# One softmax over tokens' logits for eight blocks, formed from a stash of the turned logits

## The chip, the cores and the metric

The kernel runs on one core of a Trainium2 chip. The metric is the device time of one execution in microseconds; lower is better. The inputs lie in the chip's memory when the time starts, and the output has to be there when it ends.

## What is computed

Three layers, one behind the other. Attention with a decay: 4 batches, 8 heads, 576 positions, 64 columns a head; the scores get the difference of running sums of log f, a causal mask, a softmax and the product with v. Then a feed-forward layer on the 2304 tokens of 512 columns, `g = h * sigmoid(1.702 h)` with `h = x @ w_in` (512 to 2048), and `g @ w_out`. Then a layer of soft experts on its output x:

```
logits = x @ phi                          # 2304 x 32
d = softmax(logits) over the tokens       # each slot's weights
slot_input = d.T @ x                      # 32 slots, 4 for each of 8 experts
slot_out = relu(slot_input @ w1) @ w2     # each expert on its own 4 slots
c = softmax(logits) over the 32 slots     # each token's weights
out = c @ slot_out                        # 2304 x 512
```

Everything is float32 on the way in and out. The change concerns `c`, the softmax of each token over the 32 slots.

## The kernel before

The 2304 tokens are 18 blocks of 128 (`NBLK`), taken two at a time as 9 chunks (`NCH`). `attn_items` lists the steps of attention (scores, exponentials, product with v, turning x) with a place and a modelled cost each; the main part (from L1063) runs the feed-forward layer chunk by chunk in `moe_steps`, and behind each of its steps `attend` emits as many attention items as the modelled costs allow. So attention for later chunks and the feed-forward layer of earlier ones stand side by side. Of the whole program a scheduler then draws up one fixed order for each engine from modelled times (L1282); each engine works off its list in order, and semaphores hold an instruction until its inputs and its buffer are there. A tile with one buffer (`bufs=1`) waits until the tile before it on that tag has had its last use.

In attention's later rows (`emit_qk`, L538) TensorE forms scores (L551, L552, L562, L566), VectorE their maximum (L574), ScalarE the exponential (L578) and a half-precision copy (L586), VectorE the remainder of it (L587), and SP issues a DMA that turns the two (`ph`, L591). `emit_pv` multiplies the turned exponentials with v on TensorE (L628 to L630).

In `moe_steps` TensorE forms `hp` (L800 to L802), ScalarE and VectorE make `g` of it (L813, L814), and `turn` transposes g (L756), copies it (L763) and multiplies it by `wphi`, which is w_out times phi (`by_phi`, L778). These sums of a chunk lie in PSUM on the tag "mi", which has one buffer. When a chunk's sums are complete, `slot_steps` begins, and each step of the next chunk's `moe_steps` drives it on to its next `yield`:

1. VectorE copies the sums out as `l4` (L845). TensorE multiplies by `rsum`, which adds up the four partial sums, in two ways into one tile `lg` on the tag "mi": L853 gives the logits turned (`lT`, slots on partitions, tokens on columns; the 32 slots stand four times, once in each quarter of the partitions), and `by_token` (L856) gives them with tokens on partitions, one matmul of 32 columns for each block.
2. The softmax over tokens goes on from `lT` with a running maximum: `nm` (L881 to L884), exponential `dT` (L885).
3. `token_softmax` (L862) forms `c` for the chunk's two blocks from the logits with tokens on partitions: maximum (L865), subtraction (L866), exponential on ScalarE (L867), sum (L869), a small addition and reciprocal (L870, L871), product into `csm` (L873).
4. After three more steps `dT` is turned back (L896, L898) and weighs g into `spart` (L921, L928).

The last chunk is handled a block at a time (`ts` is one block), and its second block (`end`) does `by_token` and `token_softmax` last of all.

When attention is done, its memory becomes a ring of tiles (`ring`), and SP begins to load the expert weights into it (`load_e`, L1051, L1053, L1056); tiles of the feed-forward layer join the ring as they come free. After the last chunk, `slots_in` (L942) multiplies the slot sums by w_out (L954). `ct_steps` (L979) turns `csm` eight blocks at a time; the first two parts of it are made ahead. `zi` (L1139), the reciprocal sums of the slots, has the tag "rm", two buffers, like the maxima of `token_softmax`; it is read by the ReLU of L1179. The experts' second product `so` (L1194, L1207) uses two PSUM tiles, the second of them on the tag "mi" (L1187), cleared by VectorE (L1189). L1240 multiplies it with the turned `c`, and the output leaves by DMA.

Of the kernel before, what the change touches and what calls it, by code (L numbers as in the profile page):

```python
# [10 lines left out]
F32 = mybir.dt.float32  # L11
# [3 lines left out]
AF = mybir.ActivationFunctionType  # L15
ALU = mybir.AluOpType
AX = mybir.AxisListType
# [13 lines left out]
def attention_moe_softmoe(ctx, tc, q, k, v, f, w_in, w_out, phi, w1, w2, out):  # L31
    nc = tc.nc
# [4 lines left out]
    NS = phi.shape[1]  # L37
# [11 lines left out]
    NCH = NBLK // 2  # L49
# [3 lines left out]
    mp = ctx.enter_context(tc.tile_pool(name="mp", bufs=1))  # L53
# [20 lines left out]
    ident = const.tile([128, 128], F32, name="ident")  # L74
# [16 lines left out]
    zst = const.tile([128, 1], F32, name="zst")  # L91
    spart = mp.tile([128, 512], F32, tag="spart", name="spart")
    csm = const.tile([128, NBLK, NS], F32, name="csm")

    def setup_consts():
        make_identity(nc, ident)
# [730 lines left out]
    def warm(k):  # L827
# [5 lines left out]
        for _ in range(k):  # L833
# [3 lines left out]
                )  # L837
            )

    def slot_steps(c, ts=(0, 1)):  # L840
        fresh = c == 0
        nt = len(ts)
        end = c == NCH - 1 and ts[-1] == 1
        l4 = mp.tile([128, 256], F32, tag="l4", name="l4", bufs=1)[:, 0:128 * nt]
        nc.vector.tensor_scalar(  # L845
            out=l4, in0=P4.pop((c, ts[0]))[:, 0:128 * nt], scalar1=1.0 / (GS * WS), scalar2=None, op0=ALU.mult
        )
        lg = ps_mi("lg")
        lT = lg[:, 0:128 * nt]
        lgv = lg[:, 256:256 + nt * NS].rearrange("p (t s) -> p t s", t=nt)  # L850
# [3 lines left out]
        def by_token():  # L854
            for i in range(nt):
                nc.tensor.matmul(lgv[:, i, :], lhsT=l4[:, 128 * i:128 * (i + 1)], rhs=rsum[:, 0:NS], start=True, stop=True)  # L856

        if not end:
            by_token()
        yield  # L860

        def token_softmax():  # L862
            rm = mp.tile([128, 2, 1], F32, tag="rm", name="rm", bufs=2)[:, 0:nt]
            ee = mp.tile([128, 2, NS], F32, tag="ee", name="ee", bufs=1)[:, 0:nt]
            nc.vector.tensor_reduce(out=rm, in_=lgv, axis=AX.X, op=ALU.max)  # L865
            nc.vector.tensor_tensor(out=ee, in0=lgv, in1=rm.to_broadcast([128, nt, NS]), op=ALU.subtract)  # L866
            nc.scalar.activation(out=ee, in_=ee, func=AF.Exp)  # L867
            rs = mp.tile([128, 2, 1], F32, tag="rs", name="rs", bufs=2)[:, 0:nt]
            nc.vector.tensor_reduce(out=rs, in_=ee, axis=AX.X, op=ALU.add)  # L869
            nc.vector.tensor_scalar(out=rs, in0=rs, scalar1=1e-9, scalar2=None, op0=ALU.add)  # L870
            nc.vector.reciprocal(out=rs, in_=rs)  # L871
            b0 = 2 * c + ts[0]
            nc.vector.tensor_tensor(  # L873
                out=csm[:, b0:b0 + nt, :], in0=ee, in1=rs.to_broadcast([128, nt, NS]), op=ALU.mult
            )


        nm = mp.tile([128, 2], F32, tag="nm", name="nm", bufs=2)
# [7 lines left out]
        if not fresh:  # L886
            nc.scalar.activation(out=nm[:, 1:2], in_=nm[:, 1:2], func=AF.Exp)
        yield
        if not end:
            token_softmax()  # L890
            for _ in range(3):
                yield
        pd = ps_mm("d")
# [7 lines left out]
        if end:  # L901
            sp, pt = (ps_mm("sp"), ps_sc("sp")), (ps_mm("spT"), ps_sc("spT"))
            sT = sums[0] = mp.tile([128, 512], F32, tag="gt", name="sT", bufs=N_GT)
            for n, v in enumerate(halves):
                for fg in range(FG):
                    nc.tensor.matmul(
                        sp[n][NS * fg:NS * (fg + 1), v], lhsT=dd, rhs=G[c, 1, fg][:, v], start=True, stop=True
                    )
            warm(1)
            for n, v in enumerate(halves):  # L910
                nc.vector.scalar_tensor_tensor(
                    out=spart[:, v], in0=spart[:, v], scalar=nm[:, 1:2], in1=sp[n][:, v], op0=ALU.mult, op1=ALU.add
                )
                for a in (2 * n, 2 * n + 1):
                    nc.tensor.transpose(pt[n][:, a * 128:(a + 1) * 128], spart[:, a * 128:(a + 1) * 128], ident)
                (nc.scalar.copy, nc.vector.tensor_copy)[n](out=sT[:, v], in_=pt[n][:, v])
        else:
            sp = ps_mm("sp")
            for i, t in enumerate(ts):
                for fg in range(FG):  # L920
                    nc.tensor.matmul(  # L921
                        sp[NS * fg:NS * (fg + 1), :], lhsT=dd[:, NS * i:NS * (i + 1)], rhs=G[c, t, fg],
                        start=(i == 0), stop=(i == nt - 1),
                    )
            if fresh:
                nc.vector.tensor_copy(spart, sp)
            else:
                nc.vector.scalar_tensor_tensor(  # L928
                    out=spart, in0=spart, scalar=nm[:, 1:2], in1=sp, op0=ALU.mult, op1=ALU.add
                )  # L930
        nc.vector.tensor_copy(nmst, nm[:, 0:1])
        if not fresh:
            nc.vector.scalar_tensor_tensor(
# [2 lines left out]
        yield  # L936
        if end:
            by_token()
            token_softmax()
            yield  # L940

    def slots_in():  # L942
# [121 lines left out]
    if True:  # L1064
# [71 lines left out]
        load_e(KF - 5)  # L1136
        nc.gpsimd.memset(hz, 0.0)

        zi = mp.tile([128, 2], F32, tag="rm", name="zi", bufs=2)  # L1139
        pz = ps_mm("pz")  # L1140
        for hf in range(2):
            for g in range(4):
# [144 lines left out]
```

## Time and profile before

| | us |
|---|---|
| three runs | 566.05, 561.09, 562.74; median 562.74 |
| the profiled execution, its time | 562.1 |
| its span, first to last instruction | 560.4 |
| busy: TensorE, VectorE, ScalarE, GpSimd | 506.8, 354.5, 309.2, 69.0 |
| mean granted TensorE clock, share of full | 0.973 |

The profile is of one execution. Busy time of TensorE is an upper figure, since matmuls are pipelined and their ends are modelled; weight loads (PEld) are listed apart and overlap with matmuls. An instruction on float32 appears in two passes, each with a weight load and a matmul. "Idle before" is the time in which an engine stood still just ahead of an instruction, and "<-" names what released it.

### The profile page before, as it was taken

Reading aid. Unit: us, or ns where it says so; the run is one execution under the profiler, and the core shown is the slowest. Engines: PE = TensorE matmul, PEld = TensorE weight load, DVE = VectorE, ACT = ScalarE, POOL = GpSimd, SP = SyncE. Lnnn points to the kernel's source line nnn. Section 1 sums busy time; section 2 is a strip of 40 time slices with the busy share of each in tenths; the row PEclk is TensorE's granted clock in tenths of the full one; section 3 lists DMA queues with packets and bytes.
Section 4 is the critical chain, followed back from the end, with each engine's and each line's share of the span. In section 5 each row is a group of like instructions: output and inputs, shape, how many; then the busy total and the mean of one; then the engine's idle time right before and its main releaser. Section 6 shows DMA issues by size and latency. Waiting matters only on the chain.

```text
span 560.4 us, 13652 instructions
## 1 busy us (share of the span) xinstructions
PE 506.8 (90%) x5387; PEld 317.4 (57%) x5387; DVE 354.5 (63%) x934; ACT 309.2 (55%) x604; POOL 69.0 (12%) x120
## 2 busy tenths in 40 slices
PE   3566999998989999999999799989999999899991
PEld 3455876775666555665665466546566545454431
DVE  8988969787667357577776667866764413352022
ACT  6767786786767354565666566756564233312111
POOL 4866743310000000000000000000000000000000
PEclk9879799998999999999999899999999999999997
DMA  9997674999867227996759979995544199999999
GB/s 241 275 363 173 171 126 151 262 183 190 153 130 121 58 39 146 181 182 99 130 99 151 154 139 155 208 163 104 85 78 79 37 344 369 363 341 338 379 294 284
DMA packets 229823, 105.63 MB, mean 188 GB/s; under 512 B 202592, under 2 KB 211296, under 8 KB 229760
## 3 DMA queue, kind: packets, MB, share of 16 engines
q1 hardware_dynamic: 228528, 103.59, 80.0%
q10 hardware_dynamic: 1232, 1.18, 0.7%
q8 instruction: 42, 0.69, 0.5%
q14 instruction: 21, 0.17, 0.1%
HBM read 64.63 MB, written 4.72 MB: 124 GB/s over the span
## 4 chain that ended last, share of the span: by engine, by line
PE 70%; DMA 12%; DVE 8%; ACT 5%; issue 2%; SPq 2%; ACTq 0%; DVEq 0%
PE hp L800 10%; PE hp L801 9%; PE hp L802 9%; DMA ph<-pn 6%; PE gT L756 5%; PE p L778 4%; PE pv L623 3%; PE pv L628 3%; PE l L1172 3%; PE sp L921 2%; DMA kf<-in_k_dram 2%; PE scs L551 2%; DMA we<-in_moe_w_dram 2%; PE scs L552 2%; PE pv L630 2%
## 5 line engine op out<-in xcount | busy, mean ns | idle before, releaser
L800 PE MATMUL hp<-w,xt 128*128 128x512 f16 x288 | 110.4, 383 | 0.3 <-DVE spart L928 0.3
L801 PE MATMUL hp<-w,xt 128*128 128x512 f16 x288 | 109.8, 381 | 0.0
L802 PE MATMUL hp<-w,xt 128*128 128x512 f16 x288 | 109.7, 381 | 0.0
L578 ACT ACTIVATE pf<-scs,mx 128x512 f32<-128x512 f32 (+3 forms) x108 | 57.6, 541 | 40.9 <-DVE mx L574 31.7
L814 DVE SCALAR_TENSOR_TENSOR g<-g,hp 128x512 f32<-128x512 f32 x72 | 49.2, 683 | 41.6 <-ACT g L813 40.9
L813 ACT ACTIVATE g<-hp 128x512 f32<-128x512 f32 x72 | 42.6, 591 | 51.6 <-PE hp L802 46.4
L587 DVE SCALAR_TENSOR_TENSOR pn<-pf,pn 128x512 f16<-128x512 f32 (+2 forms) x78 | 51.0, 657 | 31.0 <-ACT pn L586 30.4
L586 ACT ACTIVATE pn<-pf 128x512 f16<-128x512 f32 (+2 forms) x78 | 47.0, 606 | 26.3 <-DMA ph<-pn 25.0
L628 PE MATMUL pv<-vv,ph 128*128 128x65 f16 (+2 forms) x360 | 45.9, 199 | 7.9 <-DMA ph<-pn 7.7
L574 DVE CUSTOM_DVE_ANT_0 scs<-scs,zmq 128x128 f32<-128x128 f32 (+3 forms) x96 | 46.6, 495 | 9.1 <-PE scs L552 6.9
L802 PEld LDWEIGHTS <-xt 128*128 128x128 f16 x288 | 28.3, 98 | 33.3 <-issue 0.6
L763 ACT COPY gt<-gT 128x512 f32<-128x512 f32 x71 | 41.1, 583 | 9.7 <-PE gT L756 9.3
L628 PEld LDWEIGHTS <-ph 128*128 128x128 f16 (+2 forms) x360 | 34.4, 102 | 20.0 <-DMA ph<-pn 10.2
L629 PE MATMUL pv<-vv,ph 128*128 128x65 f16 (+2 forms) x360 | 45.3, 196 | 0.0
L756 PE MATMUL gT<-ident,g 128*128 128x128 f32 x288 | 45.1, 277 | 0.0
L630 PE MATMUL pv<-vv,ph 128*128 128x65 f16 (+2 forms) x360 | 45.1, 195 | 0.0
L800 PEld LDWEIGHTS <-xt 128*128 128x128 f16 x288 | 28.8, 100 | 27.8 <-issue 4.7
L756 PEld LDWEIGHTS gT<-ident,g 128*128 128x128 f32 x288 | 33.9, 142 | 14.4 <-issue 5.0
L801 PEld LDWEIGHTS <-xt 128*128 128x128 f16 x288 | 28.3, 98 | 22.7 <-issue 0.7
L629 PEld LDWEIGHTS <-ph 128*128 128x128 f16 (+2 forms) x360 | 34.7, 103 | 1.9 <-issue 0.2
L551 PE MATMUL scs<-kab,qa 128*128 128x128 f16 x240 | 35.2, 220 | 0.4 <-ACT pf L578 0.4
L585 POOL MEMSET pn<- 128x128 f16 x12 | 2.5, 210 | 267.3 <-DMA ph<-pn 165.8
(226 smaller groups left out, 1036.3 us busy)
## 6 DMA issues: line engine op xcount, KB each, us to landing
we<-in_moe_w_dram SPq DMA_DIRECT2D x127, 256.0 KB, 5.6
raw<-in_moe_w_in_dram SPq DMA_DIRECT2D x16, 512.0 KB, 7.3
raw<-in_moe_w_out_dram SPq DMA_DIRECT2D x16, 512.0 KB, 6.0
kf<-in_k_dram SPq DMA_DIRECT2D x13, 256.0 KB, 3.7
qf<-in_q_dram SPq DMA_DIRECT2D x13, 256.0 KB, 4.1
vf<-in_v_dram SPq DMA_DIRECT2D x12, 256.0 KB, 4.4
out_dram<-ob SPq DMA_DIRECT2D x12, 256.0 KB, 3.2
ph<-pn SPq DMA_TRANSPOSE x78, 3.3
```

Source lines behind the costliest of these rows:

```text
L574: nc.vector.tensor_tensor_reduce(out=o, in0=o, in1=mask, scale=-SC, scalar=3.0e38 if n == 128 else DG[r][1][:, u], op0=ALU.add, op1=ALU.mi ...
L578: nc.scalar.activation(out=pf[:, hh * nb:(hh + 1) * nb], in_=o, func=AF.Exp, bias=mx[:, hh:hh + 1], scale=-1.0)
L586: nc.scalar.activation(out=pn[:, 0, 0:w], in_=pf, func=AF.Copy, scale=PB)
L587: nc.vector.scalar_tensor_tensor(out=pn[:, 1, 0:w], in0=pf, scalar=PB, in1=pn[:, 0, 0:w], op0=ALU.mult, op1=ALU.subtract)
L628: nc.tensor.matmul(o, lhsT=ph[0:rr, 0, off:off + n], rhs=vh, start=(j == 0), stop=False)
L629: nc.tensor.matmul(o, lhsT=ph[0:rr, 0, off:off + n], rhs=vl, start=False, stop=False)
L630: nc.tensor.matmul(o, lhsT=ph[0:rr, 1, off:off + n], rhs=vh, start=False, stop=(j == i))
L756: last_turn[0] = nc.tensor.transpose((pt if a < 2 else pt2)[:, a * 128:(a + 1) * 128], g[:, a * 128:(a + 1) * 128], ident)
L800: nc.tensor.matmul(hp, lhsT=xt[:, 0, kk, ts], rhs=win(0, fg, kk), start=(kk == 0), stop=False)
L801: nc.tensor.matmul(hp, lhsT=xt[:, 0, kk, ts], rhs=win(1, fg, kk), start=False, stop=False)
L802: last_hp[0] = nc.tensor.matmul(hp, lhsT=xt[:, 1, kk, ts], rhs=win(0, fg, kk), start=False, stop=(kk == KD - 1))
L814: nc.vector.scalar_tensor_tensor(out=g, in0=g, scalar=1.0, in1=hp, op0=ALU.add, op1=ALU.mult)
```

## The change

For chunks 0 to 7 the logits with tokens on partitions are no longer made by `by_token`. Instead ScalarE copies one quarter of the turned logits `lT`, 32 partitions by 256 columns, into a tile `stash` of 128 partitions: chunk c into quarter c % 4. After every fourth chunk (c = 3 and 7) `token_softmax_8` turns the stash with two 128x128 transposes, each of which writes its 128 columns in four runs of 32, into one PSUM tile (on the tag "mi" the first time, on "sc" the second), and runs one softmax over all eight blocks. It is emitted behind `spart` of that chunk. The last chunk's two blocks stay as they were. The exponential is now formed in place in `csm`, and the tags "rm" and "rs" have one buffer each, wider than before; `zi`, which shares "rm", has one buffer too. The number of steps that `slot_steps` yields is unchanged.

```diff
--- before.py
+++ after.py
@@ -91,6 +91,7 @@
     zst = const.tile([128, 1], F32, name="zst")
     spart = mp.tile([128, 512], F32, tag="spart", name="spart")
     csm = const.tile([128, NBLK, NS], F32, name="csm")
+    stash = mp.tile([128, 256], F32, tag="stash", name="stash")
 
     def setup_consts():
         make_identity(nc, ident)
@@ -837,9 +838,32 @@
                 )
             )
 
+    def token_softmax(b0, nt, lgv):
+        rm = mp.tile([128, 8, 1], F32, tag="rm", name="rm", bufs=1)[:, 0:nt]
+        ee = csm[:, b0:b0 + nt, :]
+        nc.vector.tensor_reduce(out=rm, in_=lgv, axis=AX.X, op=ALU.max)
+        nc.vector.tensor_tensor(out=ee, in0=lgv, in1=rm.to_broadcast([128, nt, NS]), op=ALU.subtract)
+        nc.scalar.activation(out=ee, in_=ee, func=AF.Exp)
+        rs = mp.tile([128, 8, 1], F32, tag="rs", name="rs", bufs=1)[:, 0:nt]
+        nc.vector.tensor_reduce(out=rs, in_=ee, axis=AX.X, op=ALU.add)
+        nc.vector.tensor_scalar(out=rs, in0=rs, scalar1=1e-9, scalar2=None, op0=ALU.add)
+        nc.vector.reciprocal(out=rs, in_=rs)
+        nc.vector.tensor_tensor(
+            out=ee, in0=ee, in1=rs.to_broadcast([128, nt, NS]), op=ALU.mult
+        )
+
+    def token_softmax_8(b0):
+        pl = (ps_mi if b0 == 0 else ps_sc)("lt")[:, 0:8 * NS]
+        for t in range(2):
+            nc.tensor.transpose(
+                pl.rearrange("p (g t s) -> p t g s", t=2, s=NS)[:, t], stash[:, 128 * t:128 * (t + 1)], ident
+            )
+        token_softmax(b0, 8, pl.rearrange("p (b s) -> p b s", s=NS))
+
     def slot_steps(c, ts=(0, 1)):
         fresh = c == 0
         nt = len(ts)
+        one = c == NCH - 1
         end = c == NCH - 1 and ts[-1] == 1
         l4 = mp.tile([128, 256], F32, tag="l4", name="l4", bufs=1)[:, 0:128 * nt]
         nc.vector.tensor_scalar(
@@ -855,24 +879,12 @@
             for i in range(nt):
                 nc.tensor.matmul(lgv[:, i, :], lhsT=l4[:, 128 * i:128 * (i + 1)], rhs=rsum[:, 0:NS], start=True, stop=True)
 
-        if not end:
+        if one and not end:
             by_token()
+        if not one:
+            gs = slice(NS * (c % 4), NS * (c % 4 + 1))
+            nc.scalar.copy(out=stash[gs], in_=lT[gs])
         yield
-
-        def token_softmax():
-            rm = mp.tile([128, 2, 1], F32, tag="rm", name="rm", bufs=2)[:, 0:nt]
-            ee = mp.tile([128, 2, NS], F32, tag="ee", name="ee", bufs=1)[:, 0:nt]
-            nc.vector.tensor_reduce(out=rm, in_=lgv, axis=AX.X, op=ALU.max)
-            nc.vector.tensor_tensor(out=ee, in0=lgv, in1=rm.to_broadcast([128, nt, NS]), op=ALU.subtract)
-            nc.scalar.activation(out=ee, in_=ee, func=AF.Exp)
-            rs = mp.tile([128, 2, 1], F32, tag="rs", name="rs", bufs=2)[:, 0:nt]
-            nc.vector.tensor_reduce(out=rs, in_=ee, axis=AX.X, op=ALU.add)
-            nc.vector.tensor_scalar(out=rs, in0=rs, scalar1=1e-9, scalar2=None, op0=ALU.add)
-            nc.vector.reciprocal(out=rs, in_=rs)
-            b0 = 2 * c + ts[0]
-            nc.vector.tensor_tensor(
-                out=csm[:, b0:b0 + nt, :], in0=ee, in1=rs.to_broadcast([128, nt, NS]), op=ALU.mult
-            )
 
 
         nm = mp.tile([128, 2], F32, tag="nm", name="nm", bufs=2)
@@ -886,8 +898,9 @@
         if not fresh:
             nc.scalar.activation(out=nm[:, 1:2], in_=nm[:, 1:2], func=AF.Exp)
         yield
+        if one and not end:
+            token_softmax(2 * c + ts[0], nt, lgv)
         if not end:
-            token_softmax()
             for _ in range(3):
                 yield
         pd = ps_mm("d")
@@ -928,6 +941,8 @@
                 nc.vector.scalar_tensor_tensor(
                     out=spart, in0=spart, scalar=nm[:, 1:2], in1=sp, op0=ALU.mult, op1=ALU.add
                 )
+        if c % 4 == 3:
+            token_softmax_8(2 * c - 6)
         nc.vector.tensor_copy(nmst, nm[:, 0:1])
         if not fresh:
             nc.vector.scalar_tensor_tensor(
@@ -936,7 +951,7 @@
         yield
         if end:
             by_token()
-            token_softmax()
+            token_softmax(2 * c + ts[0], nt, lgv)
             yield
 
     def slots_in():
@@ -1136,7 +1151,7 @@
         load_e(KF - 5)
         nc.gpsimd.memset(hz, 0.0)
 
-        zi = mp.tile([128, 2], F32, tag="rm", name="zi", bufs=2)
+        zi = mp.tile([128, 2], F32, tag="rm", name="zi", bufs=1)
         pz = ps_mm("pz")
         for hf in range(2):
             for g in range(4):
```

## Rows read from the trace of the kernel before

**Rows 1.** Stretches: us, busy us (instructions) of each engine, clock, DMA share, GB/s.
```profile
460.00:480.00 20.00, 19.32 (x141) 9.95 (x140) 6.16 (x19) 5.89 (x14) 0.00 (x0) 1.00 1.03 371
...
sum 285.00, PE 277.24 PEld 168.82 DVE 188.61 ACT 166.61 POOL 3.61; mean PE 19.80 PEld 12.06 DVE 13.47 ACT 11.90 POOL 0.26
```

**Rows 2.** SP's queue: timeline (start, length in us), and one of its waits.
```profile
445.77 41.91 SPq L1051 DMA_DIRECT2D we<-in_moe_w_dram  x60
...
502.88 0.33 SPq L1053 DMA_DIRECT2D hz<-in_moe_w_dram  x1
...
SPq L1053 <- PE sw L954: 3.6, 2, 3.2
```

**Rows 3.** Waits of PE between 160 and 445 us: us in total, times, longest.
```profile
PE pv L628 <- DMA ph<-pn: 7.4, 8, 2.0
```

**Rows 4.** Timeline of weight loads around L856 in chunks 2 and 6.
```profile
247.16 0.63 PEld L856 LDWEIGHTS lg<-rsum,l 128*128 128x128 f32 x4
247.63 0.50 PEld L756 LDWEIGHTS gT<-ident,g 128*128 128x128 f32 x4
248.10 0.10 PEld L800 LDWEIGHTS <-xt 128*128 128x128 f16 x1
...
432.93 0.63 PEld L856 LDWEIGHTS lg<-rsum,l 128*128 128x128 f32 x4
433.60 0.10 PEld L630 LDWEIGHTS <-ph 64*64 64x64 f16 x1
```

**Rows 5.** Groups by line and shape: one chunk's softmax (busy us, mean ns | idle before).
```profile
L867 ACT ACTIVATE ee<-ee 128x64 f32<-128x64 f32 x8 | 2.0, 256 | 1.3 <-DVE ee L866 1.3
...
L873 DVE TENSOR_TENSOR csm<-ee,rs 128x64 f32<-128x64 f32 x8 | 1.8, 220 | 0.1
...
L865 DVE TENSOR_REDUCE rm<-lg 128x2 f32<-128x64 f32 x8 | 1.7, 218 | 0.3 <-ACT dT L885 0.3
...
L870 DVE TENSOR_SCALAR rs<-rs 128x2 f32<-128x2 f32 x8 | 1.3, 166 | 0.2
```

**Rows 6.** Groups by line and shape: instructions on 256 columns.
```profile
L885 ACT ACTIVATE dT<-lg,nm 128x256 f32<-128x256 f32 x8 | 3.7, 468 | 9.8 <-DVE nm L883 7.5 <-PE scs L552 2.4
...
L881 DVE TENSOR_REDUCE nm<-lg 128x1 f32<-128x256 f32 x8 | 3.4, 421 | 3.9 <-PE lg L856 3.9
L845 DVE TENSOR_SCALAR l<-p 128x256 f32<-128x256 f32 x8 | 3.4, 419 | 0.9 <-PE p L778 0.9
...
L258 ACT COPY part<-wq 128x256 f32<-128x256 f32 x8 | 2.9, 369 | 1.1 <-PE wq L253 1.0
```

**Rows 7.** The tail: timelines of DVE and ACT, and a wait from 500 us on.
```profile
506.29 0.16 DVE L1148 TENSOR_SCALAR zi<-pz 128x2 f32<-128x2 f32 x1 [1.18 <-PE pz L1144]
506.37 0.18 DVE L865 TENSOR_REDUCE rm<-lg 128x1 f32<-128x32 f32 x1
...
523.71 0.69 ACT L1179 ACTIVATE g<-l,zi 128x512 f32<-128x512 f32 x1 [3.51 <-PE l L1172]
...
PEld so L1207 <- DMA we<-in_moe_w_dram: 2.8, 5, 0.7
```

**Rows 8.** Stretches of 5 us around the largest hole (columns as in rows 1).
```profile
305.00:310.00 5.00, 4.06 (x64) 2.54 (x59) 3.95 (x8) 4.14 (x9) 0.00 (x0) 1.00 0.54 104
310.00:315.00 5.00, 4.40 (x76) 3.00 (x73) 3.17 (x10) 3.42 (x7) 0.00 (x0) 1.00 0.60 116
315.00:320.00 5.00, 3.02 (x32) 1.44 (x31) 3.96 (x9) 1.47 (x3) 0.00 (x0) 0.85 1.23 152
320.00:325.00 5.00, 5.00 (x55) 2.91 (x55) 2.18 (x5) 4.00 (x9) 0.20 (x1) 0.81 1.16 211
```

**Rows 9.** Timeline of DVE behind the sums of chunk 3.
```profile
298.33 0.74 DVE L928 SCALAR_TENSOR_TENSOR spart<-spart,nm,sp 128x512 f32<-128x512 f32 x1
...
305.31 0.69 DVE L587 SCALAR_TENSOR_TENSOR pn<-pf,pn 128x512 f16<-128x512 f32 x1 [2.78 <-ACT pn L586]
```

## Prediction

> **What bounds the kernel now.** I read the busy time by stretches first [rows 1]. Between 160 and 445 us, where the feed-forward chunks and the attention run interleaved, TensorE is busy for 277.2 of 285.0 us; VectorE for 188.6 (66%) and ScalarE for 166.6 (58%). From 460 to 480 us TensorE is still at 19.3 of 20, and DMA now runs at its full share (1.03, 371 GB/s), because the expert weights load. So what is to be asked of every edit is what it does to TensorE's issue, and whether the weight loads behind it let the gain through.
>
> They do, by the queue of SP [rows 2]. The first expert load is issued at 445.77 us, once attention is done. Near the end the queue stops: it waits 3.6 us for the matmuls of L954, and the load behind them goes out at 502.88. L954 can only run when the last chunk's sums are ready, so the loads after 502.88 follow TensorE, not only DMA. A shift of TensorE before 500 us moves both the start of the loads and this stop, and with it the end.
>
> Next the waits of TensorE within 160 to 445 us: the only one that counts is L628 on the turned exponentials `ph`, 7.4 us in 8 places [rows 3]. The rest is issue. TensorE is the bound there, with a few holes.
>
> **The change, part by part.** The sum is made against the profiled execution's own time, 562.1 us (a span of 560.4 and 1.7 around it). The median of the three runs shown is 562.74, 0.6 higher, inside their spread of 5.
>
> *TensorE, removed.* For each of the chunks 0 to 7 the two matmuls of L856 go. Each appears as two passes, so a group has four weight loads. From the first load of a group to the next instruction's load pass 247.63 - 247.16 = 0.47 us for chunk 2 and 433.60 - 432.93 = 0.67 us for chunk 6 [rows 4]. The other six groups read 0.47 five times and 0.67 once. Removed: 6 x 0.47 + 2 x 0.67 = 4.16 us. This is what the weight loads take; 32 columns stream in less.
>
> *TensorE, added.* Two 128x128 transposes for four chunks, four in all. L756 is the same operation: four of them from 247.63 to 248.10, 0.47 us [rows 4]. Added: 0.47 us. From below it is 0, if the loads go beside a running matmul; from above I allow twice the row, 0.94, since no row has a transpose that scatters its output in runs of 32 columns. I take 0.47, the row itself.
>
> The Trainium skill speaks against this part: its page "PSUM — Partial Sum Buffer", section "Specifications (TRN2)", says that any non-contiguous access pattern slows matmuls significantly. It gives no factor, and no row here shows such a write; an estimate by it, with the four transposes taking twice as long, makes the net gain 3.2 us.
>
> Net on TensorE: -4.16 + 0.47 = -3.7 us.
>
> *VectorE.* The softmax of one chunk has two reductions (0.218 us, L865), two elementwise steps (0.220, L873) and two small ones (0.166, L870) [rows 5]: 1.21 us, eight times 9.7 us. The one for eight blocks works on 128x256: reductions as L881 (0.421) and elementwise as L845 (0.419) [rows 6], 2 x 0.421 + 2 x 0.419 + 2 x 0.166 = 2.01 us, twice 4.0. VectorE loses 5.7 us, beside TensorE. I count it as nothing; at best it shortens the holes of [rows 3] (rival A).
>
> *ScalarE.* Eight exponentials of 0.256 us go [rows 5]; two of 0.468 (as L885) and eight stash copies come. A copy has 32 partitions of 256 columns; the nearest row is L258, 0.369 us for 128 partitions of as many columns [rows 6]. In all -2.05 + 0.94 + 2.95 = +1.8 us, on an engine that is 58% busy. The copy stands ahead of the exponential L885 on ScalarE, but L885 itself idles 9.8 us over its eight times, 7.5 of it for the maximum on VectorE [rows 6]; the copy fits there. Without that cover it would delay L885 by up to 0.37 us a chunk, 3.0 in all; I take 0.
>
> *New waits.* First, the turned stash of the first four chunks takes the single "mi" bank, which the running sums of the next chunk (L778) and its logits also need. Whoever comes after it waits for two transposes, one reduction and one subtraction: 0.24 + 0.421 + 0.419 = 1.1 us. Behind a waiting L778 on TensorE stand transposes and feed-forward matmuls that need nothing from it, and the order is drawn up so that ready ones go first. Between 0 and 1.1; I take 0. Before, the same bank was held through the old reads of L865 and L866 in every chunk, so something is given back. Second, the copy of chunk 4 overwrites the stash and must wait for the first two transposes, which are short: 0. Third, the tag "rm" now has one buffer and `zi` uses it. `zi` is written at 506.29 and read until the last L1179 ends, 523.71 + 0.69 = 524.40 [rows 7]. The last block's maximum L865, now at 506.37, would come after it, and its bank is the one that the second half of `so` is cleared in. With three VectorE steps of about 0.2 us (as L865 there) the second half starts near 525.0 instead of 524.2. That 0.8 us is covered: L1207 still waits 2.8 us for weights on the way [rows 7]. If TensorE stood still for the whole last softmax as well (another 1.2 us by rows 5, and the splits), it would be some 2.5 us, just under that cover. I take 0, and keep 2.5 as the end of the range for it.
>
> **Sum:** 562.1 - 4.16 + 0.47 = 558.4; I say 558.5 us. What is late next is the same TensorE stream, 3.7 us earlier.
>
> **The rivals.** A, more is won: VectorE has 5.7 us less to do in the stretches where the chain maximum, exponential, split, `ph` decides. For it speak the 7.4 us of holes [rows 3], and that the worst of them, 305 to 320 us (5 - 4.06, 5 - 4.40 and 5 - 3.02, 3.5 us idle), also brings the granted clock to a mean of 0.85 and 0.81 of 2.4 GHz over the next two 5 us, that is part of the time at 1.2 GHz, some 0.75 + 0.95 = 1.7 us more [rows 8]. Against it: most of these holes end with a DMA, which VectorE only starts. Half of 7.4 + 1.7 won: 558.5 - 4.5 = 554.0.
>
> B, less is won: what the first six chunks save (5 x 0.47 + 0.67 = 3.0) is time in which TensorE arrives earlier at the same holes and waits longer. Then only the last two groups count, 0.67 + 0.47 - 0.24 = 0.9: 561.2. For it: the `ph` of a hole goes through SP's queue among the row loads, which don't move with TensorE. Against it: the scores that begin each of these chains are TensorE's own and come earlier too.
>
> C, slower: the first softmax for eight blocks lands in front of the worst hole. Its place in the program is right behind `spart` of chunk 3, at 298.33 us; on VectorE it takes 0.421 + 0.419, then the exponential's 0.468, then 0.421 + 0.332 + 0.419, 2.5 us from end to end. VectorE waits 2.78 us before the split L587 at 305.31 [rows 9]. Started before 302.8 it fits in; from there on each 0.1 us is 0.1 us of L587, of the `ph` behind it, and of TensorE in the hole. In full: 2.5, the 1.1 of the bank, and once more the 1.7 of lower clock [rows 8]: 558.5 + 5.3 = 563.8. Against it: the four softmaxes before it are gone, so the items arrive earlier.
>
> **How the numbers follow.** My forecast gets 0.50, A 0.20, B 0.15, C 0.15. A run of this kernel can tell about 1% (5.6 us) from no change. Faster by more than that is below 556.5: most of A (0.17) and the low edge of the forecast (0.06), 0.23. Slower by over 1% is above 567.7: only C with a second hole of the same kind (another 5.2 us, 3.5 + 1.7), and what a newly drawn order might do elsewhere: 0.09. The rest, 0.68, is within 1%. The forecast's own range is 556 to 561: doubled transposes and the bank (+1.6), up to 2.5 at the end if its cover goes, and down to where a hole closes. To hold 8 in 10 the range takes in most of A and of C: 553.5 to 565.5.
>
> **What would show it.** L856 down from 36 to 4 passes; L865 to L873 under new lines with four executions each (two wide, two narrow); 32-partition copies of some 0.37 us on ScalarE; the first expert load near 442.5 instead of 445.77, the load after L954 near 499.2 instead of 502.88. If both shift by 3 to 4 us and the end doesn't, the reading of the tail is wrong. If the first load doesn't shift, B is right; if the waits of L628 in 160 to 445 us fall under 4 us, A; if they rise over 10, C. The last maximum should stand after 524 us less the shift, with no wait of L1194 that reaches the output. The prediction is wrong if TensorE's groups were not worth 0.47 us each, which the gap from L853 to its successor would show.

## The result, and the profile after

The changed kernel takes 555.21 us in the median of six runs (551.72 to 558.32), the kernel before 563.48 in six runs beside it. The ratio is 0.9859, with an interval of 0.9829 to 0.9888: faster by 1.4%, that is by 8 us, where I had forecast 3.6 us, a chance of 0.68 for "within 1%" and of 0.23 for more. The profiled execution took 555.42 us, with a span of 553.3. Of the runs below, the profiled ones of e1 and e10 took 590 and 1213 us, where their others took 550 to 563, and one of e11 took 1.6% more than its fastest; these three are left out of all numbers.

The tail did as forecast. Timeline of SP's queue, kernel after; the two rows answer to [rows 2]:

```profile
438.18 1.79 SPq L1066 DMA_DIRECT2D we<-in_moe_w_dram  x4
...
495.19 0.33 SPq L1068 DMA_DIRECT2D hz<-in_moe_w_dram  x1
```

The first expert load goes out 7.6 us earlier, the load behind the stop 7.7 earlier, the span ends 7.1 earlier. So the whole gain was made before 438 us and the tail handed it on. The late maximum of the last block came as described, in the timeline of VectorE (kernel after; [rows 7]):

```profile
516.73 0.19 DVE L844 TENSOR_REDUCE rm<-lg 128x1 f32<-128x32 f32 x1
```

A wait of TensorE after 500 us, kernel after:

```profile
PEld so L1222 <- DMA we<-in_moe_w_dram: 2.9, 5, 0.7
```

It runs at 516.73 instead of 506.37, behind the last ReLU, and `so` still waits for its weights as long as before (2.9 us against 2.8): the cover held.

The new instructions cost what their neighbours did. Groups of the kernel after by line, VectorE's and ScalarE's first; they answer to [rows 4 to 6]:

```profile
L844 DVE TENSOR_REDUCE rm<-lt 128x8 f32<-128x256 f32 x2 | 0.8, 419 | 0.0
L845 DVE TENSOR_TENSOR csm<-lt,rm 128x256 f32<-128x256 f32 x2 | 0.8, 418 | 0.0
L886 ACT COPY stash<-lg 32x256 f32<-32x256 f32 x8 | 2.9, 363 | 5.8 <-PE lg L877 5.8
```

And the transposes of the octets (the softmaxes over eight blocks) beside those of g, with min/median/max in ns (kernel after). Unlike the matmuls of L856, a float32 transpose appears in one pass:

```profile
L858 PEld LDWEIGHTS lt<-ident,stash x4: 138/141/144, 332.9 to 464.8; 128*128 128x128 f32 x4
L858 PE MATMUL lt<-ident,stash x4: 272/272/328, 332.9 to 464.9; 128*128 128x128 f32 x4
...
L757 PEld LDWEIGHTS gT<-ident,g x288: 137/141/224, 109.5 to 486.6; 128*128 128x128 f32 x144
L757 PE MATMUL gT<-ident,g x288: 272/273/329, 109.7 to 486.7; 128*128 128x128 f32 x144
```

Predicted were 0.421, 0.419 and 0.369 us for the first three. Now the stretch of attention, by 5 us, columns as in [rows 1, 8] (kernel after):

```profile
305.00:310.00 5.00, 3.92 (x52) 2.59 (x51) 3.06 (x7) 3.20 (x6) 0.00 (x0) 1.00 0.55 105
310.00:315.00 5.00, 5.00 (x77) 3.20 (x75) 4.02 (x11) 3.60 (x7) 0.00 (x0) 1.00 0.93 134
315.00:320.00 5.00, 5.00 (x90) 3.41 (x88) 3.42 (x9) 3.21 (x7) 0.21 (x1) 1.00 0.75 147
320.00:325.00 5.00, 4.87 (x37) 2.41 (x35) 3.29 (x9) 3.21 (x7) 0.00 (x0) 1.00 1.25 202
```

TensorE's waits between 160 and 445 us, kernel after:

```profile
PE pv L629 <- DMA ph<-pn: 5.1, 5, 1.5
PE hp L801 <- DVE g L815: 0.7, 1, 0.7
PE lg L877 <- DVE l L869: 0.7, 1, 0.7
```

The worst hole of before is gone: 1.2 us idle in these 20, against 3.5, and the clock is whole. But one of 1.5 us stands just behind, at 326 us, where the kernel before has none between 325 and 330. The waits on `ph` fell from 7.4 to 5.1 us, between my marks for rival A (under 4) and rival C (over 10). TensorE's timeline shows that hole and the place of the third wait (kernel after):

```profile
326.36 0.20 PE L629 MATMUL pv<-vv,ph 128*128 128x65 f16 x1 [1.50 <-DMA ph<-pn]
...
377.91 0.70 PE L877 MATMUL lg<-l,rsum 128*128 128x256 f32 x2 [0.72 <-DVE l L869]
```

The third wait is for the sums of chunk 5, and has nothing to do with the first octet, which VectorE's timeline shows some 40 us earlier, behind the sums of chunk 4:

```profile
330.15 0.41 DVE L869 TENSOR_SCALAR l<-p 128x256 f32<-128x256 f32 x1
...
334.02 0.42 DVE L844 TENSOR_REDUCE rm<-lt 128x8 f32<-128x256 f32 x1
...
334.95 0.42 DVE L845 TENSOR_TENSOR csm<-lt,rm 128x256 f32<-128x256 f32 x1
...
338.80 0.41 DVE L851 TENSOR_TENSOR csm<-csm,rs 128x256 f32<-128x256 f32 x1
```

The octet of chunks 0 to 3 did not run behind chunk 3's `spart` (rival C's place) but at 334 us. It is strung out over 5 us between attention's items, so it holds nothing up for 2.5 us at a stretch. Between 327 and 377 us TensorE has no wait of half a microsecond, so the "mi" bank that the octet holds cost nothing to be seen.

**Where the time went.** I cut the span at two instructions that both kernels have: the copy `l4` (L845, after L869) of chunk 0 and that of chunk 7. Stretches, first of the kernel before, then of the kernel after:

```profile
170.03:466.46 296.43, 289.25 (x3105) 173.54 (x3103) 188.43 (x539) 167.24 (x336) 3.61 (x30) 0.99 0.72 134
```

```profile
169.00:458.87 289.87, 283.74 (x3079) 169.74 (x3078) 184.36 (x503) 167.31 (x337) 3.57 (x30) 1.00 0.72 138
```

1.0 us was gained before chunk 0, ahead of every changed instruction; 6.6 between the cuts; 0.5 was given back behind them. Of the 6.6, idle time of TensorE (length less busy) is 7.18 - 6.13 = 1.1. The low clock of [rows 8] cost 3.02 x 0.15 + 5.00 x 0.19 = 1.4 before and nothing after. The rest, 289.25 - 1.4 - 283.74 = 4.1, is work at full clock; forecast for the seven groups between the cuts, less one octet's transposes, was 3.3 to 3.5. So the groups are there, and some 2.5 us come from holes and clock, which the sum had at zero.

### The profile page after: what moved, and what is told of

It is laid out like the page before. It is cut to its first block, busy times and chain, and to the rows that moved or that the text cites. A ratio compares the mean times of both kernels' runs of the same rounds, so it can differ in the third digit from the quotient of the medians.

```text
span 553.3 us, 13559 instructions
## 1 busy us (share of the span) xinstructions
PE 500.3 (90%) x5359; PEld 313.1 (57%) x5359; DVE 350.8 (63%) x898; ACT 310.3 (56%) x606; POOL 69.8 (13%) x120
## 4 chain that ended last, share of the span: by engine, by line
PE 66%; DMA 14%; DVE 9%; ACT 5%; issue 3%; SPq 2%; ACTq 0%; POOL 0%; DVEq 0%; POOLq 0%
PE hp L801 9%; PE hp L802 8%; PE hp L803 8%; PE gT L757 5%; DMA ph<-pn 4%; PE p L779 4%; PE pv L624 3%; DMA we<-in_moe_w_dram 3%; PE pv L629 3%; PE l L1187 3%; PE sp L934 2%; DMA kf<-in_k_dram 2%; PE scs L552 2%; DMA kab<-kan 2%; PE scs L553 2%
## 5 line engine op out<-in xcount | busy, mean ns | idle before, releaser
L757 PE MATMUL gT<-ident,g 128*128 128x128 f32 x288 | 45.0, 276 | 0.0
L629 PEld LDWEIGHTS <-ph 128*128 128x128 f16 (+2 forms) x360 | 34.1, 101 | 18.2 <-DMA ph<-pn 8.0
L757 PEld LDWEIGHTS gT<-ident,g 128*128 128x128 f32 x288 | 34.2, 141 | 14.7 <-issue 4.4
L631 PEld LDWEIGHTS <-ph 128*128 128x128 f16 (+2 forms) x360 | 34.7, 103 | 1.7 <-issue 1.4
L630 PEld LDWEIGHTS <-ph 128*128 128x128 f16 (+2 forms) x360 | 34.5, 102 | 2.0 <-issue 0.2
```

The source lines that it names most:

```text
L629: nc.tensor.matmul(o, lhsT=ph[0:rr, 0, off:off + n], rhs=vh, start=(j == 0), stop=False)
L630: nc.tensor.matmul(o, lhsT=ph[0:rr, 0, off:off + n], rhs=vl, start=False, stop=False)
L631: nc.tensor.matmul(o, lhsT=ph[0:rr, 1, off:off + n], rhs=vh, start=False, stop=(j == i))
L757: last_turn[0] = nc.tensor.transpose((pt if a < 2 else pt2)[:, a * 128:(a + 1) * 128], g[:, a * 128:(a + 1) * 128], ident)
```

## The experiments

The question: does TensorE's term hold when it is the only change, and what opened or closed the holes: the softmax's work on VectorE or ScalarE, its place, the bank, or merely the order that the scheduler drew up? Every edit makes it draw a new one. Ratios are to the kernel before, timed on the same chip; the brackets hold 95% intervals. Each profile is of one execution. Of e1 and e10 only the times are used.

**Matmuls alone (e1, e1b).** The kernel before without the groups of L856; the softmax reads turned logits.

```diff
-        if not end:
+        one = c == NCH - 1
+        if one and not end:
             by_token()
+        if not one:
+            lgv = lg[:, 0:nt * NS].rearrange("p (t s) -> p t s", t=nt)
```

> The kernel before without the matmuls of by_token in chunks 0 to 7; the softmax of these chunks runs with all its instructions on the first 64 columns of the turned logits instead, so c is formed from other numbers there. SP's order differs from before in 2 lines only. Theory 'issue' (the weight loads of the removed matmuls, 0.47 us a group, are time on TensorE; 4.2 us in all): 4.2 us less than before, ratio 0.9925, within 1.5 us. Theory 'relief' (the gain comes from VectorE's shorter work): nearly nothing, under 1 us. Theory 'groups cost more' (the removed matmuls explain all of the change): 7 to 9 us less, ratio 0.985.

> The same kernel as e1_no_matmul, once more for a profile: the kernel before without the by_token matmuls of chunks 0 to 7 (the softmax reads the first 64 columns of the turned logits instead, so the weights of the tokens are other numbers). Theory 'terms': the matmuls are worth their issue time alone, 0.47 to 0.67 us a group, 4.2 us in all, ratio 0.992 to 0.996, and the waits of TensorE on the turned exponentials between 160 and 445 us stay near the 7.4 us of before. Rival 'matmuls close the holes': these waits fall under 4 us and the ratio is near the whole change's, 0.986.

Measured: 0.9952 [0.9919, 0.9986], and again 0.9966 [0.9939, 0.9992]: 1.9 to 2.7 us, the second just past the upper edge of "terms". The stretch between the cuts and two of 5 us (e1b):

```profile
169.70:464.17 294.47, 285.57 (x3077) 170.14 (x3075) 187.04 (x540) 165.70 (x336) 3.57 (x30) 0.99 0.75 135
...
365.00:370.00 5.00, 2.14 (x28) 1.40 (x27) 3.12 (x7) 3.65 (x8) 0.00 (x0) 0.97 1.00 186
370.00:375.00 5.00, 5.00 (x39) 2.67 (x37) 1.94 (x7) 1.83 (x4) 0.00 (x0) 0.68 0.82 108
```

TensorE's waits between the cuts (e1b):

```profile
PE pv L628 <- DMA ph<-pn: 5.4, 6, 1.5
PE scs L551 <- ACT pf L578: 1.6, 2, 1.4
```

Busy time at full clock falls by 3.9 us (285.57 less 1.7 of low clock, against 287.85), which is the forecast of the groups. But idle rises from 7.18 to 8.90: `ph` is waited for a little less (6.8 before), the scores' bank and others more. So by the profile half of it is given back; by the times the gain may be anything from 0.4 to 4.6 us. That is rival B's mechanism, and matmuls alone don't close holes.

**Matmuls back (e3).** The kernel after with the groups in all chunks again, read by nobody.

```diff
-        if one and not end:
+        if not end:
             by_token()
```

> The changed kernel with the matmuls of by_token in all chunks again, their results unused in chunks 0 to 7. Theory 'issue plus order' (3.7 us of the gain are TensorE's issue, the rest comes from the order that the scheduler happened to draw between 283 and 430 us): SP's order is here nearer to that of before (8 lines differ) than to that of the changed kernel (24), so both parts of the gain go: ratio to before 0.995 to 1.003. Theory 'relief' (VectorE's 5.7 us less): only the matmuls' 4.2 us come back, ratio 0.993. Theory 'groups cost more': all of the gain goes, ratio 1.00, by the matmuls alone, and then the run without them has it all.

Measured: 0.9868 [0.9831, 0.9904], below what all three theories had. By this ratio the groups are hardly seen (0.9859 without them, intervals of 0.3% on both sides). But the kernel before got faster in the course of that chip's runs, from 562.8 to 565.6 us in the first seven to 560.1 to 562.1 in the other ten; against the median of all seventeen, e3's median gives 0.9917, and the groups would be worth some 3 us. By the profile they are seen (e3, between the cuts):

```profile
170.34:462.42 292.08, 286.60 (x3107) 173.23 (x3106) 184.94 (x503) 167.65 (x337) 3.57 (x30) 1.00 0.68 136
```

286.60 - 283.74 = 2.9 us for 28 more passes, seven groups of 0.41. Idle is 5.5, less than in the kernel after. So with all the old matmuls in place half of the gain or more stays, and that part hangs on the softmax, not on the groups.

**The softmax's place (e4).** The kernel before, with each chunk's softmax emitted behind its `spart`.

```diff
         if not end:
-            token_softmax()
             for _ in range(3):
                 yield
...
+        if c < NCH - 1:
+            token_softmax()
         nc.vector.tensor_copy(nmst, nm[:, 0:1])
```

> The kernel before with the softmax of each chunk moved in the program from behind the exponential of the turned logits to behind the slot sums; nothing is left out. SP's order is that of before, TensorE's differs in 5 lines. Theory 'issue plus order': no change, ratio 0.998 to 1.002. Theory 'place' (the softmax stood in front of attention's maxima and splits on VectorE, and the changed kernel gains because it no longer does): 2 to 4 us less, ratio 0.993 to 0.996.

Measured: 1.000 [0.997, 1.003]. This change of place makes no difference. Between the cuts, and around the old hole (e4):

```profile
169.64:466.06 296.42, 287.91 (x3105) 173.05 (x3104) 188.65 (x539) 167.16 (x336) 3.57 (x30) 1.00 0.73 134
...
305.00:310.00 5.00, 4.04 (x54) 2.33 (x54) 3.67 (x8) 4.06 (x8) 0.00 (x0) 1.00 0.50 97
310.00:315.00 5.00, 4.40 (x82) 3.21 (x80) 3.36 (x10) 3.38 (x6) 0.00 (x0) 1.00 0.59 113
315.00:320.00 5.00, 2.54 (x44) 1.57 (x39) 3.71 (x8) 1.91 (x4) 0.00 (x0) 1.00 1.11 125
```

The hole of [rows 8] is there again, 4.0 us against 3.5, but at full clock.

**The bank (e8).** The kernel after, with the turned stash in the "mm" bank both times.

```diff
-        pl = (ps_mi if b0 == 0 else ps_sc)("lt")[:, 0:8 * NS]
+        pl = ps_mm("lt")[:, 0:8 * NS]
```

> The changed kernel with the turned stash in a bank of the tag mm (three buffers) both times, instead of the single bank of mi and one of sc; nothing is left out. SP's order here is nearer to that of before (12 lines differ) than to that of the changed kernel (26). Theory 'issue plus order': the direct part stays, 3.7 us, the part that came with the order goes, ratio to before 0.992 to 0.995. Theory 'relief': the work is that of the changed kernel, ratio 0.986. If the wait for the single bank in chunk 4 cost something in the changed kernel, this one is faster than it by up to 1.1 us.

Measured: 0.9866 [0.9823, 0.991], against 0.9859. The 1.1 us that I had allowed for the "mi" bank cannot be seen.

**VectorE's steps alone (e9), ScalarE's alone (e10).** The kernel after with six more VectorE steps of a chunk's softmax in each of the chunks 0 to 7, or with its exponential, written to scratch.

```diff
+        if not one:
+            lv = lg[:, 0:nt * NS].rearrange("p (t s) -> p t s", t=nt)
+            nc.vector.tensor_reduce(out=rx, in_=lv, axis=AX.X, op=ALU.max)
+            nc.vector.tensor_tensor(out=ex, in0=lv, in1=rx.to_broadcast([128, nt, NS]), op=ALU.subtract)
+            nc.vector.tensor_reduce(out=ry, in_=ex, axis=AX.X, op=ALU.max)
...
```

```diff
+        if not one:
+            nc.scalar.activation(out=ex, in_=lg[:, 0:nt * NS].rearrange("p (t s) -> p t s", t=nt), func=AF.Exp)
```

> The changed kernel with six more VectorE instructions a chunk in chunks 0 to 7, of the kinds, the sizes and the place of the old softmax, on the turned logits, into a tile that nobody reads; no exponential. TensorE's and SP's orders stay close to those of the changed kernel (4 lines of SP's differ). Theory 'relief', by VectorE: 3 to 4.5 us of the gain go, ratio to before 0.992 to 0.994. Theory 'order': the time of the changed kernel, ratio 0.985 to 0.988.

> The changed kernel with the eight exponentials of 64 columns on ScalarE again, at the old place, into a tile that nobody reads. SP's order is that of the changed kernel. Theory 'relief', by VectorE, and theory 'order': the time of the changed kernel, ratio 0.985 to 0.988. Theory 'relief', by ScalarE: 2 to 4 us of the gain go, ratio 0.990 to 0.993.

Measured: e9 0.988 [0.984, 0.9919], e10 0.9812 [0.9762, 0.9861]. Eight more exponentials take nothing away. VectorE's steps take 1.2 us by time, with some 2.8 either way; the one profiled execution has more (e9, between the cuts and two stretches of 5 us):

```profile
169.36:462.83 293.47, 285.01 (x3079) 170.19 (x3078) 189.24 (x545) 167.56 (x337) 3.56 (x30) 0.99 0.71 135
...
220.00:225.00 5.00, 2.91 (x47) 2.00 (x46) 3.13 (x7) 3.29 (x7) 0.20 (x1) 1.00 0.74 137
225.00:230.00 5.00, 5.00 (x34) 2.48 (x32) 2.21 (x5) 1.56 (x4) 0.20 (x1) 0.66 0.90 196
```

Idle is back to 8.5, and a hole of 2.1 us is followed by 1.7 us of low clock. The profile suggests "relief" by VectorE, but the times lie below its 0.992 to 0.994, at the edge of "order".

**Everything back (e11).** The kernel after with the matmuls and the whole softmax chain, exponential included, in the chunks 0 to 7 beside the new octets. It is e3 plus the chain.

```diff
-        if one and not end:
+        if not end:
             by_token()
...
+        if not one:
+            nc.vector.tensor_reduce(out=rx, in_=lgv, axis=AX.X, op=ALU.max)
+            nc.vector.tensor_tensor(out=ex, in0=lgv, in1=rx.to_broadcast([128, nt, NS]), op=ALU.subtract)
+            nc.scalar.activation(out=ex, in_=ex, func=AF.Exp)
+            nc.vector.tensor_reduce(out=ry, in_=ex, axis=AX.X, op=ALU.add)
...
```

> The kernel after with all that the change took out put back beside the new: both matmuls of by_token and the whole softmax chain over VectorE and ScalarE in each of the chunks 0 to 7, written to a scratch tile. Theory 'work': the removed work as a whole made time and holes, so everything gained is lost: ratio 0.999 to 1.004, waits on the turned exponentials back to 6 us or more. Theory 'order': only TensorE's groups come back, 3.5 us, and the holes stay as small as in the kernel after unless the order drawn up puts others there: 0.988 to 0.994.

Measured: 0.9994 [0.9961, 1.0027]. All that was gained is lost again, as "work" has it, though the waits on `ph` (below) stay under the 6 us that I had named with it. From e3 to e11, where TensorE's matmuls are the same, that is 1.26%, 7 us, with some 2.8 either way (4 us by the plain medians). The stretch between the cuts (e11):

```profile
170.46:465.29 294.83, 286.20 (x3107) 173.35 (x3106) 189.66 (x546) 169.67 (x345) 3.57 (x30) 1.00 0.72 135
```

TensorE's waits there (e11):

```profile
PE pv L629 <- DMA ph<-pn: 5.6, 6, 1.5
PE scs L552 <- ACT pf L579: 1.0, 2, 0.7
```

TensorE's work is e3's (286.2 against 286.6); its idle time goes from 5.5 to 8.6. Work and idle time together are 2.7 us more than in e3. The profiled execution was 1.3 us faster than e11's median, and that of e3 0.9 slower than its own, so they show less of the loss than the times.

**No softmax (e2, e2b), and nothing at all (e7, e7b).** The kernel before without the softmax of chunks 0 to 7; the kernel after without stash and octets. Both need `csm` filled with something: by GpSimd at the very start in e2 and e7, by one VectorE step at chunk 8 in e2b and e7b.

```diff
-        if not end:
+        if c == NCH - 1 and not end:
             token_softmax()
+        if not end:
             for _ in range(3):
```

```diff
-        if not one:
-            gs = slice(NS * (c % 4), NS * (c % 4 + 1))
-            nc.scalar.copy(out=stash[gs], in_=lT[gs])
...
-        if c % 4 == 3:
-            token_softmax_8(2 * c - 6)
```

> The kernel before with its matmuls of by_token, but without the per-chunk softmax over tokens in chunks 0 to 7 (48 instructions on VectorE, 8 on ScalarE; csm is zero there). Theory 'relief' (the gain beyond TensorE's own 3.7 us comes from the softmax work that leaves VectorE and ScalarE): 4 to 7 us less than before, ratio 0.988 to 0.993. Theory 'order' (it comes from the order that happens to be drawn): this one has an order of its own, 38 lines of SP's differ from before, and the ratio may lie anywhere from 0.990 to 1.005.

> The changed kernel without the stash copies, the four transposes and the two softmaxes of eight blocks: chunks 0 to 7 have no softmax over tokens at all, csm is zero there. What the added parts cost is the difference to the changed kernel. Theory 'issue plus relief': the transposes' 0.5 us and a share of 4.0 us of VectorE, 1 to 3 us less than the changed kernel, ratio to before 0.980 to 0.985. If the added parts are hidden altogether: ratio 0.985 to 0.988.

> As e2_no_softmax (before without the softmax of chunks 0 to 7, matmuls kept), but the rows of csm are filled at chunk 8 by one VectorE instruction from spart, not at the start by GpSimd, so that the first 170 us are those of before. Theory 'relief' (VectorE's and ScalarE's softmax work makes the holes): the chunk sums of chunk 0 to 7 come closer together by 3 to 4 us and the ratio is 0.990 to 0.994. Theory 'order' (holes go with the order drawn up, not with the work): holes of the size of before somewhere, ratio 0.997 to 1.006, and the loss of e2 from chunk 0 on shows again. If e2 was slow only by its first 170 us: below 1.002.

> As e7_none (neither matmuls nor softmax nor stash for chunks 0 to 7), filled at chunk 8 by VectorE. If e7's first 170 us were lost to its GpSimd fill alone: ratio 0.981 to 0.986, the whole change's or a little less, since the octets' own work is 0.5 us of TensorE. If the fill had no part in it: 0.993 to 0.995 as e7. Less than 0.981 would say that the octets and stash copies cost more than their rows.

Measured: e2 1.0105 [1.0076, 1.0134] and e7 0.9941 [0.991, 0.9972], with chunk 0's `l4` at 175.0 and 176.3 us instead of 170.0 and 169.0. With the fill at chunk 8 instead, e2b is 0.9998 [0.9969, 1.0026] and e7b 0.98 [0.9747, 0.9854], the fastest kernel here along with e10. So e2b loses little in its first 170 us (chunk 0's `l4` at 171.6) and yet gains nothing, against "relief". Between the cuts and two stretches of 5 us (e2b):

```profile
171.61:467.92 296.31, 288.13 (x3105) 174.38 (x3103) 184.26 (x498) 165.57 (x329) 3.57 (x30) 0.99 0.72 134
...
370.00:375.00 5.00, 1.67 (x27) 1.48 (x26) 5.00 (x14) 3.68 (x8) 0.00 (x0) 0.74 0.74 129
375.00:380.00 5.00, 5.00 (x34) 3.15 (x34) 2.94 (x10) 2.36 (x5) 0.00 (x0) 0.58 0.57 64
```

TensorE's waits between the cuts (e2b):

```profile
PE pv L628 <- DMA ph<-pn: 3.6, 5, 1.6
PE pv L628 <- DVE x L642: 3.3, 1, 3.3
```

VectorE's timeline ahead of L642 (e2b):

```profile
371.05 0.28 DVE L328 COPY qan<-qbn 64x512 f16<-64x512 f16 x1
...
371.35 0.65 DVE L329 TENSOR_TENSOR qbn<-qf,qbn 64x512 f16<-64x512 f32 x1
371.92 0.68 DVE L353 SCALAR_TENSOR_TENSOR vv<-vf,vv 64x512 f16<-64x512 f32 x1
372.53 0.54 DVE L587 SCALAR_TENSOR_TENSOR pn<-pf,pn 128x384 f16<-128x384 f32 x1
373.00 0.41 DVE L642 TENSOR_TENSOR x<-pv,rd 128x256 f32<-128x256 f32 x1
```

The waits on `ph` did fall, to 3.6 us. But one new hole stands at 370 us. VectorE is busy for 5.00 of 5: the order now puts the splits of the next row's q and v (and of its k, just before) ahead of L642, the step that TensorE's next product with v waits for. That is 3.3 us of wait and 2.5 of low clock (1.67 x 0.26 + 5.00 x 0.42). Taken off in full, these 5.8 us would put e2b at 0.9895 by estimate, near e3. That may be too much: the profiled run took 563.5 us, the longest of ten with a median of 561.9, and its mean granted clock of 0.965 is the lowest among them, which one other run shares. And between the cuts (e7b):

```profile
167.48:452.76 285.28, 282.22 (x3077) 169.10 (x3076) 183.53 (x496) 165.28 (x329) 3.57 (x30) 1.00 0.70 140
```

TensorE's waits there (e7b):

```profile
PE pv L629 <- DMA ph<-pn: 1.4, 2, 1.2
```

The holes are smallest in the kernel in which VectorE has least to do.

**All of them side by side.** "Work" is TensorE's busy time between the cuts less what the low clock cost, "lost" the idle time and that cost, both in us and from one profiled execution.

| kernel | groups in | chunk's softmax in | ratio | work | lost |
|---|---|---|---|---|---|
| before | yes | yes | 1 | 287.9 | 8.6 |
| e4 | yes | yes | 1.000 | 287.9 | 8.5 |
| e11 | yes | yes | 0.9994 | 286.2 | 8.6 |
| e1b | no | yes | 0.9966 | 283.9 | 10.6 |
| e9 | no | VectorE's steps | 0.988 | 283.3 | 10.2 |
| e2b | yes | no | 0.9998 | 285.6 | 10.7 |
| e3 | yes | no | 0.9868 | 286.6 | 5.5 |
| after | no | no | 0.9859 | 283.7 | 6.1 |
| e8 | no | no | 0.9866 | 283.0 | 4.7 |
| e7b | no | no | 0.98 | 282.2 | 3.1 |

Work goes with the groups alone: 286.8 in the mean of the five with them, 283.2 without. Lost time goes with the softmax of each chunk: 8.5 to 10.6 in the five that have it, 3.1 to 6.1 in four of the five that don't. The fifth is e2b, with its one misplaced hole. By time e9 belongs to the other side, with 0.988. Work also differs by 2.3 us between the kernel before and e2b, which have the same matmuls; differences of a microsecond in one profile carry nothing.

## Why the prediction was right, and where it wasn't

The time came out inside the range of 553.5 to 565.5 only because the range took in most of rival A; the forecast's own range, 556 to 561, lies above it. The forecast itself, 558.5, had less than half of the gain: TensorE's term was right, and a second one of 4 to 7 us was put at nothing.

**What bounds the kernel: right.** TensorE is at 98% between the cuts, and the first expert load, the stop behind the last chunk's sums and the end moved together by 7.6, 7.7 and 7.1 us.

**TensorE, removed and added: right.** The work read is 4.1 us lower from before to after, 3.9 in e1b, 2.9 in e3 the other way round, 3.6 in the mean of the table, where the forecast between the cuts was 3.3 to 3.5. The row of 0.47 us for a group that takes four weight loads held, though loads overlap with matmuls elsewhere. What the step left out is that the groups by themselves seem to pay only half (1.9 to 2.7 us by time, with intervals up to 4.6), since TensorE then waits longer in the holes. I had this as rival B, at 0.15.

The Trainium skill's "PSUM — Partial Sum Buffer", section "Specifications (TRN2)", says that a pattern with gaps slows matmuls significantly. The transposes that write in four runs of 32 take 272 ns in the median and their loads 141; those of L757, which write without gaps, take 273 and 141 in the median of the same run. In these four, runs of 32 columns, 128 bytes, cost nothing that can be seen.

**VectorE "beside TensorE. I count it as nothing", ScalarE "I take 0": here the sum failed.** The softmax out of each chunk, on the two engines together, is half of the gain or more. Put back beside the same matmuls (e3 to e11) it takes 7 us with 2.8 either way (4 by the plain medians), which brings the kernel back to the time of before; from e1b to the kernel after, 0.9966 to 0.9859, it is 6 with 2.2 either way. That VectorE was busy for 66% of the stretch doesn't make its work free: TensorE's holes end with a `ph` whose chain runs through VectorE [rows 3, 9]. Rival A came nearest in time, at 554.0; I gave it 0.20 because the holes end with a DMA. But its mechanism, VectorE's shorter work, is not shown: VectorE's steps alone take 1.2 us by time, with 2.8 either way, though 4.0 of lost time in one profile (e9), and the waits on `ph` stayed above my mark for it.

What part of the chain does it, and how, is not settled. Its exponentials on ScalarE alone take nothing (e10), nor does its place (e4). How VectorE and ScalarE hand over to each other within the chain was not tried by itself. Nor does the softmax stand close ahead of any large hole in the kernel before: its six holes of over 0.5 us begin 16 us or more behind the last step of a chunk's softmax. Ahead of the worst of them: VectorE's last step of chunk 3's softmax and its next long wait, ScalarE's copy ahead of the split of [rows 9], and the hole itself on TensorE (timelines, kernel before):

```profile
291.61 0.22 DVE L873 TENSOR_TENSOR csm<-ee,rs 128x64 f32<-128x64 f32 x1
...
295.50 0.29 DVE L322 COPY kan<-kbn 128x512 f16<-128x512 f16 x1 [2.18 <-ACT kbn L318]
...
304.65 0.63 ACT L586 ACTIVATE pn<-pf 128x512 f16<-128x512 f32 x1 [3.78 <-DMA ph<-pn]
...
316.99 0.21 PE L628 MATMUL pv<-vv,ph 128*128 128x65 f16 x1 [1.98 <-DMA ph<-pn]
```

In between VectorE idles 2.2 us and, in [rows 9], 2.8 us, each time for ScalarE, and ScalarE 3.8 us for an earlier DMA. So it is no queue of VectorE's work that reaches from the softmax to this hole.

Work and order can't be parted wholly, since each edit draws a new order, and e2b shows that a lighter kernel can be drawn worse. In some pairs they nearly are. Of the 862 instructions that VectorE has in every version (all but those of the softmax over the slots), in the order in which the traces show them, 115 stand elsewhere in the kernel after than in the kernel before, but only 14 in e11 than in e3, 29 in e9 and 3 in e10 than in the kernel after. So it is likelier the chain's work than a new order that costs e11 its time; no single instruction was shown to make the 2.5 us of holes and clock that went.

**The 1.7 us of low clock in rivals A and C** were tied to the hole at 305 us. e4 has that hole and a whole clock, so the hole by itself doesn't bring them. Of the 7.1 us between the two profiles 1.4 are low clock all the same.

**Bank, stash, "rm", ScalarE by itself: taken as nothing, and nothing shows.** e10 with eight exponentials more is no slower; the bank can't be seen (e8); the late maximum cost nothing. Stash, octets and their work together are 3.3 us by time, with 3.4 either way (e7b against after, 0.98 and 0.9859): a cost of that size is neither shown nor excluded.

**Rival C: fell**, since the octet was not drawn behind `spart` of chunk 3 (at 301 us in the kernel after) but 33 us later, and in pieces.

## What to carry to other kernels

An engine that is busy two thirds of the time need not be free if the bounding engine's holes are fed through it: price the removed work once at nothing and once at the holes that its chain ends in, and give the second a real chance. Where a scheduler draws the order from modelled times, test an edit by putting its work back beside the new version as well as by taking it from the old; each version is one draw, and a lighter one can come out no faster (e2b); compare most closely the versions whose orders are nearly the same. Removing matmuls alone from an engine that waits elsewhere may pay only part of their time.

## What the hardware showed that I had not expected

The clock after a hole is not read off the hole's length. In e4 TensorE idles 0.96 + 0.60 + 2.46 us from 305 to 320 and the granted clock stays at 1.00; in the kernel before it idles 0.94 + 0.60 + 1.98 there and the clock means 0.85 and 0.81 over the last two 5 us. In e9 a 5 us with 2.09 idle is followed by one at 0.66, in e1b one with 2.86 idle by one at 0.68: in part of these, TensorE ran at 1.2 GHz instead of 2.4 while fully busy.

One GpSimd fill of 128x512 at the very start (e2, e7) put chunk 0's sums 5 to 7 us later, and the end with it; the same kernels with a VectorE step at chunk 8 instead were 6 to 8 us faster. The fill itself takes 0.52 us (e2). The loss goes with a lower clock: over 0 to 40 and 40 to 80 us the granted clock means 0.83 and 0.83 in e2 and 0.74 and 0.79 in e7, against 0.87 and 0.91 in the kernel before and 0.87 and 0.87 in the kernel after. Why the clock was lower was not tried.
